# Attention and a softplus layer on one core: q and k transposed by DMA, score halves merged, v in larger packets

## The chip, the cores and the metric

The kernel runs on one core of a Trainium2 chip. The metric is device time in microseconds of one execution; the profile shows one such execution with its engines: TensorE (PE, with PEld for its weight loads), VectorE (DVE), ScalarE (ACT), GpSimd (POOL) and SyncE (SP, which here only issues DMAs).

## The reference

Attention over 768 tokens for 4 batches and 8 heads of 64, where a token sees the first 8 tokens of its batch and the 96 tokens up to itself, with a bias that falls with distance; then a layer 512 to 2048, softplus, and a layer back to 512. Inputs and output are float32.

```python
scores = q @ k.T / sqrt(64)                    # per batch and head
rel = pos[:, None] - pos[None, :]
is_global, is_local = pos[None, :] < 8, (rel >= 0) & (rel < 96)
dist = where(is_global & ~is_local, 96, abs(rel))
scores = where(is_global | is_local, scores - slopes[head] * dist, -1e9)
x = softmax(scores) @ v                        # heads side by side: 3072 x 512
out = softplus(x @ w_in) @ w_out               # 512 -> 2048 -> 512
```

## The kernel before, in words

**Tiles.** The 3072 tokens are 24 blocks of 128; a block `n` attends to itself and the block before it (whose first keys are overwritten by the global ones). Two blocks are a window `w` of 256 tokens, 12 in all, three to a batch. A window's q, k and v are loaded as float32 (`q32`, `k32`, `v32`), cast to bfloat16 (`qb`, `kb`, `vb`), and q and k are transposed to `qT`, `kT`. Two tokens that follow each other in memory lie in one partition of q32 and k32 (512-byte packets); v is loaded by four DMAs of 256-byte packets, which put each token into the partition where the value matmul wants it.

**Stages.** For a half block (4 heads): `scores` (8 matmuls of 64 rows into the two banks of `s_ps`, 4 in the first block of a batch), `add_bias` on VectorE into `z`, `expo` on ScalarE into `pb`, `pv` (8 matmuls into `x_ps`), `normalize` on VectorE into `xs`. In the first four blocks the bias is added by matmuls and ScalarE reads the scores directly (`expo_early`). `xs` is transposed into `XT`: on TensorE for blocks 0 to 5 and the last two, by a DMA transpose for the others (L444). A group `g` of 256 tokens then takes 8 stages `mm1` (8 matmuls each, a bank of `h_ps`, then `softplus_exp` and `softplus_ln` on ScalarE into `g`) and 8 stages `mm2` (4 matmuls each into the two banks of `o_ps`, two for each half of the tokens, `ns`), two output copies on VectorE into `osb`, and stores.

**The order.** Nothing is scheduled by hand: a `Planner` in the file gives each stage an engine, a duration, a rank and the stages and buffers that it waits for, runs this as a list of events, and the instructions are written out in that order (`pl.plan`). Each engine, and each DMA queue, then works through its own list in order and waits by semaphores. `base(n)` is the rank of block `n`, in first-layer stages: 4n - 11 or 4n - 13. A load of window `w` from 4 on waits for a stage of group w - 3. `behind=[chain]` keeps loads in one line on SP. Until 24 us of the plan TensorE runs `filler` matmuls where it has nothing else.

**PSUM** has eight banks: 2 `s_ps`, 1 `x_ps`, 1 `tr_ps` for transposes, 2 `h_ps`, 2 `o_ps` (`alt`).

**Start.** q and k of window 0 are loaded in halves; weights are issued by GpSimd (`w_in_slice`, `w_out_slice`), slices 0 and 1 when k of window 1 has landed (`after_k`), slices 2 and 3 when k of window 2 has. SP issues the loads of windows 2 and 3 only when w_in slice 1, or 3, has landed (`after_weights`).

## Time and profile before

| what | value |
|---|---|
| median of 3 runs (lowest to highest) | 241.35 us (241.02 to 241.90) |
| profiled execution: time, span | 241.96 us, 240.2 us |
| granted TensorE clock, mean | 0.993 |
| busy: PE, PEld, DVE, ACT, POOL | 223.2, 158.3, 126.5, 153.3, 35.3 us |
| DMA packets | 67305, of them 35408 under 512 bytes |
| read from HBM, written | 27.26 MB, 6.29 MB |

The span goes from the first instruction to the last; the time of the execution is 1.8 us longer. Matmuls overlap, so the busy time of TensorE is not its time at work: the distance from one stage's start to the next one's is. A row of the chain or the timeline has its start, its length, the engine, the line of the file, what is written from what, and how many instructions were merged in it. A row of groups ends in busy time and mean nanoseconds of one, and the idle time ahead of it with what ended most of it.

### The profile page before, as it was taken

The numbers are of one execution on the slowest core, as the hardware profiler recorded it, in microseconds if no ns is written. First come the engines' busy times: TensorE is split into PE (matmuls) and PEld (weight loads), VectorE is DVE, ScalarE is ACT, GpSimd is POOL, SyncE is SP. The second block draws the span as 40 slices with busy tenths as digits, with TensorE's granted clock in tenths as the row PEclk, the third lists the DMA queues.
The fourth block names the chain that finished last, engine by engine and source line by source line (L and its number), as shares of the span: only waits on it lengthen the run. The fifth ranks groups of instructions, "written<-read, shape, count | busy, mean of one in ns | idle before, by whom it ended". The sixth has DMA issues, their size and how long they took to land.

```text
span 240.2 us, 5361 instructions
## 1 busy us (share of the span) xinstructions
PE 223.2 (93%) x2206; PEld 158.3 (66%) x2240; DVE 126.5 (53%) x260; ACT 153.3 (64%) x208; POOL 35.3 (15%) x62
## 2 busy tenths in 40 slices
PE   6889985998999979999999999999999999899994
PEld 6678664675867657767667667667667677577643
DVE  6275331379669565745665676457638537420030
ACT  4636535793688657766956866766677678568600
POOL 3252034012222021011022021012022000000000
PEclk9999998899999999999999999999999999999999
DMA  6999999999961663474781852763942302003032
GB/s 177 217 155 187 178 233 189 180 246 245 250 140 25 144 166 89 111 203 98 187 195 23 212 140 47 178 154 85 259 94 64 68 4 68 23 0 90 0 87 89
DMA packets 67305, 31.81 MB, mean 132 GB/s; under 512 B 35408, under 2 KB 64336, under 8 KB 67280
## 3 DMA queue, kind: packets, MB, share of 16 engines
q1 hardware_dynamic: 62912, 27.14, 49.2%
q0 software_dynamic: 4224, 4.19, 11.1%
q8 instruction: 17, 0.28, 0.5%
q10 hardware_dynamic: 144, 0.13, 0.2%
q14 instruction: 8, 0.07, 0.1%
HBM read 27.26 MB, written 6.29 MB: 140 GB/s over the span
## 4 chain that ended last, share of the span: by engine, by line
PE 72%; DVE 11%; DMA 7%; SPq 4%; issue 3%; ACT 1%; POOL 1%; DVEq 0%; POOLq 0%
PE h_ps L454 30%; PE o_ps L482 26%; DVE z L380 5%; PE s_ps L362 5%; PE x_ps L406 3%; DMA k_211<-in_k_dram 3%; PE tr_ps L303 3%; PE o_ps L498 3%; DMA v_593<-in_v_dram 2%; SPq L279 2%; DMA q_1345<-in_q_dram 2%; DVE osb L517 2%; PE alt_d L596 1%; SPq L282 1%; DVE qT L312 1%
## 5 line engine op out<-in xcount | busy, mean ns | idle before, releaser
L454 PE MATMUL h_ps<-XT,w_in_bf 128*128 128x256 bf16 x768 | 98.5, 275 | 0.0
L482 PE MATMUL o_ps<-w_out_bf,g 128*128 128x512 bf16 x320 | 84.9, 379 | 2.7 <-issue 0.8
L454 PEld LDWEIGHTS <-w_in_bf 128*128 128x128 bf16 x768 | 73.1, 99 | 20.0 <-issue 0.2
L464 ACT ACTIVATE e<-h_ps 128x512 f32<-128x512 f32 x96 | 56.4, 591 | 39.1 <-PE h_ps L454 38.7
L386 ACT ACTIVATE pb<-z 128x1024 bf16<-128x1024 f32 (+1 forms) x40 | 39.5, 988 | 22.1 <-DVE z L380 12.6
L468 ACT ACTIVATE g<-e 128x1024 bf16<-128x1024 f32 x48 | 50.6, 1055 | 1.3
L482 PEld LDWEIGHTS <-g 128*128 128x128 bf16 x352 | 31.8, 98 | 25.2 <-ACT g L468 0.7
L380 DVE TENSOR_TENSOR z<-s_ps,biasA 128x1024 f32<-128x1024 f32 x34 | 41.5, 1220 | 13.0 <-PE s_ps L362 9.6
L517 DVE COPY osb<-o_ps 128x512 f32<-128x512 f32 x22 | 14.9, 684 | 17.7 <-PE o_ps L482 17.5
L418 DVE TENSOR_TENSOR xs<-x_ps,rcp 128x256 bf16<-128x256 f32 x48 | 20.4, 424 | 1.7
L417 DVE RECIPROCAL rcp<-x_ps 128x4 f32<-128x4 f32 x48 | 8.5, 178 | 23.7 <-PE x_ps L406 20.4
L362 PE MATMUL s_ps<-qT,kT 64*128 64x128 bf16 x336 | 17.7, 221 | 2.0 <-DVE z L380 1.5
L406 PEld LDWEIGHTS <-pb 128*128 128x128 bf16 x320 | 14.4, 97 | 7.1 <-ACT pb L386 1.5
L362 PEld LDWEIGHTS <-kT 64*128 64x128 bf16 x352 | 10.4, 95 | 10.8 <-issue 8.2
L312 DVE COPY qT<-tr_ps 128x1024 bf16<-128x1024 bf16 x11 | 7.6, 691 | 16.6 <-PE tr_ps L303 16.6
L596 PE MATMUL alt_d<-ident 128*128 128x128 bf16 x128 | 11.6, 244 | 2.3 <-POOL ident masks.py:199 2.3
L312 DVE COPY kT<-tr_ps 128x1024 bf16<-128x1024 bf16 x11 | 7.5, 684 | 8.2 <-PE tr_ps L303 8.0
L328 POOL COPY kT<-kT 128x32 bf16<-128x32 bf16 x16 | 3.6, 223 | 52.3 <-PE s_ps L362 48.1
L596 PEld LDWEIGHTS <-ident 128*128 128x128 bf16 x128 | 9.2, 112 | 2.9 <-POOL ident masks.py:199 2.3
L303 PE MATMUL tr_ps<-ident,kb 128*128 128x128 bf16 x88 | 6.7, 219 | 3.7 <-POOL kb L292 2.7
L303 PEld LDWEIGHTS <-kb 128*128 128x128 bf16 x96 | 6.2, 98 | 4.9 <-POOL kb L292 3.0
L392 ACT ACTIVATE pb<-s_ps 128x512 bf16<-128x512 f32 (+1 forms) x12 | 5.7, 525 | 5.7 <-PE s_ps L362 5.7
(111 smaller groups left out, 140.1 us busy)
## 6 DMA issues: line engine op xcount, KB each, us to landing
out_dram<-osb SPq DMA_DIRECT2D x45, 128.0 KB, 2.5
w_in_bf<-in_moe_w_in_dram POOLq DMA_DIRECT2D x4, 512.0 KB, 7.7
w_out_bf<-in_moe_w_out_dram POOLq DMA_DIRECT2D x4, 512.0 KB, 10.0
q_123<-in_q_dram SPq DMA_DIRECT2D x2, 256.0 KB, 3.7
k_125<-in_k_dram SPq DMA_DIRECT2D x2, 256.0 KB, 4.4
v_129<-in_v_dram SPq DMA_DIRECT2D x4, 128.0 KB, 5.5
q_201<-in_q_dram SPq DMA_DIRECT2D x1, 512.0 KB, 6.3
k_211<-in_k_dram SPq DMA_DIRECT2D x1, 512.0 KB, 7.6
```

Of the source, the lines that this page charges most:

```text
L303: nc.tensor.transpose(tr[:, m - lo, r, :], src[:, r, 2 * m : 2 * m + 2, :].rearrange("p a b -> p (a b)"), ident[:],)
L362: nc.tensor.matmul(banks[sub][:, lh // 2 if i == 0 else 2 * (lh // 2) + b, :], qk_of("k", n - b)[rows, m, :], qT[rows, m, :], start=begin, ...
L380: nc.vector.tensor_tensor(z[:], s_ps[:], biasA[:, half, :, :], ALU.add)
L386: nc.scalar.activation(pb[:, 0:nr, :], z[:, 0:nr, :], AF.Exp, scale=1.0 / root_d)
L406: nc.tensor.matmul(xv[:, lh, :], pb[:, 2 * j + b, :], vb_of(n - b)[:, h, :], start=b == 0, stop=b == 1,)
L418: nc.vector.tensor_tensor(xs[:, 4 * half : 4 * half + 4, :], xv[:, :, 0:D], rcp[:][:, :, None].to_broadcast([P, 4, D]), ALU.mult,)
L454: nc.tensor.matmul(hv[:, j, :], w_in_bf[:, m, fb * P : fb * P + P], XT[:, m, W * g : W * g + W], start=(m == 0), stop=(m == NM - 1),)
L464: nc.scalar.activation(e[:, p % 2, :], state["h", g, p][:], AF.Exp)
L468: nc.scalar.activation(gt[:, 4 * c : 4 * c + 4, :].rearrange("p a t -> p (a t)"), state["e", g, c][:].rearrange("p a t -> p (a t)"), AF.Ln ...
L482: nc.tensor.matmul(state["o", g][ns][:], gt[:, fb, ns * P : ns * P + P], w_out_bf[:, fb, :], start=(fb == 0), stop=(fb == NFB - 1),)
L517: copy_on[eng](osb[:], state["o", g][ns][:])
L596: nc.tensor.matmul(alt["d"][:, 0:P], ident[:], ident[:])
```

## The change

It does four things.

1. From window 4 on (`T_DMA`) q and k are transposed by DMA (`transp_dma`), two transposes each per window, from `qb` and `kb` straight into `qT` and `kT`. k is cast by four instructions of 64 partitions that also move each token to its partition (`cast_by_block`); q keeps its two interleaved halves and is read with a step by `q_of`. Windows 0 to 3 are still transposed on TensorE, into the banks H or O.
2. v is loaded like q and k, in one DMA of 512-byte packets, and its four casts move it.
3. PSUM is dealt out anew: `s_ps` is two pairs of banks (S0, S1), `tr_ps` is gone, `o_ps` is one bank. From block 8 on (`MERGED`) both halves of a block's scores are one stage (`scores_both`), each half in a pair of its own. The second layer runs one half of the tokens after the other in the one bank (`mm2_one`); group 0's second layer runs in S1 (`mm2_first`), which therefore holds no scores meanwhile.
4. Ranks and choices of the planner follow: casts of windows 0 to 3 may go to any of three engines, casts of later windows come 4 ranks earlier, loads of a window wait for an earlier stage.

```diff
-    s_ps = ps.tile([P, 8, P], F32, name="s_ps")
+    s_ps = [ps.tile([P, 8, P], F32, name=f"s_ps{i}") for i in range(2)]
     x_ps = ps.tile([P, 512], F32, name="x_ps")
-    tr_ps = ps.tile([P, 1024], BF16, name="tr_ps")
-    alt = {x: bank(f"alt_{x}", f"bank_{x}") for x in "abcd"}
+    h_ps = [ps.tile([P, 512], F32, name=f"h_ps{i}") for i in range(2)]
+    o_ps = ps.tile([P, 512], F32, name="o_ps")
...
     def load(w, what, heads=slice(0, H)):
         b, ww = divmod(w, WPB)
-        dst = raw_of(what[0], w)
-        if what[0] == "v":
...
-            nc.sync.dma_start(dst[64 * r : 64 * r + 64, blk, :, :], vv[r])
...
+        src = {"q": q, "k": k, "v": v}[what][b, heads, W * ww : W * ww + W, :]
+        dst = raw_of(what, w)[:, heads, :]
+        nc.sync.dma_start(dst, src.rearrange("h (p r) d -> p h (r d)", r=2))
...
+    def cast_by_block(eng, w, what, blk, r):
...
+        src = raw_of(what, w)[64 * blk : 64 * blk + 64, :, r * D : r * D + D]
+        copy_on[eng](dst[64 * r : 64 * r + 64, :, :], src)
...
+    def transp_dma(w, what, i):
+        dst = q_tile(w) if what == "q" else k_tile(w)
+        nc.sync.dma_start_transpose(
+            dst[:, i, :, :], state[what + "b", w][:, i, :, :].rearrange("p h d -> p (h d)")
+        )
...
+    def q_of(n, rows, m):
+
+        b = 64 * (n % 2)
+        return state["qT", n // 2][rows, :, m, b : b + 64]
...
+    def scores_both(n):
+        scores(n, 0, s_ps[0], True)
+        scores(n, 1, s_ps[1], True)
...
+    def mm2_one(g, dst, ns, fbs):
+        for fb in fbs:
+            nc.tensor.matmul(
+                dst,
+                state["g", g][:, fb, ns * P : ns * P + P],
+                w_out_bf[:, fb, :],
+                start=(fb == 0),
+                stop=(fb == NFB - 1),
+            )
...
+    def mm2_first(p, s_t):
         for ns in range(2):
...
+            mm2_one(0, o_first(ns, s_t), ns, range(2 * p, 2 * p + 2))
...
-        {"S": 1, "X": 1, "TR": 1, "H": 2, "O": 1, "e": 3, "g": 3, "osb": 3, "z": 3, "pb": 3,
+        {"S0": 1, "S1": 1, "X": 1, "H": 2, "O": 1, "e": 3, "g": 3, "osb": 3, "z": 3, "pb": 3,
...
-    EARLY = 4
+    EARLY, MERGED, T_DMA = 4, 8, 4
...
-                if early:
+                if w < 4:
                     eng = {"pool": 1.05 * f, "act": 0.2 + 0.85 * f, "dve": 0.1 + 0.6 * f}
...
-                    u - 5.0 + 0.1 * (what == "k"),
+                    u - (5.0 if w < T_DMA else 9.0) + 0.1 * (what == "k"),
...
+                if w >= T_DMA:
+                    for i in range(2):
+                        o = pl.add(
+                            f"D{what}{w}", "sp", 1.2,
+                            lambda op, what=what, i=i: transp_dma(w, what, i), u - 19.0,
+                            after=wait, takes=takes if i == 0 else (), dma=(32, 20), slack=1.5,
+                            frees=free_b if i else (),
+                        )
...
+                elif half == 0:
+                    sc = pl.add(
+                        f"scores{n}", "pe", 2 * pe - 0.18, lambda op: scores_both(n), r,
+                        after=after, takes=(("S0",), ("S1",)),
...
             mm2s[g, p] = pl.add(
-                f"mm2_{g}_{p}", "pe", 0.865, lambda op, g=g, p=p: mm2(g, p), r,
...
+                f"mm2_{g}_{p}", "pe", 0.865,
+                lambda op, g=g, ns=ns, c=c: mm2_one(g, o_ps[:], ns, range(4 * c, 4 * c + 4)),
...
-        for what, p in (("q", 1), ("k", 1), ("v", 4)):
+        for what, p in (("q", 0), ("k", 0), ("v", 2)):
```

How the order moves is not in these lines. Three places matter for what follows. In the rows, numbers tell buffers apart; `x2` is two equal instructions in a row.

SP's queue around the loads of window 10, a middle window: first before, q and k, a half's stores, an x transpose, and v.

```order
L282 DMA q32_2382<-in_q_dram 128x8x128
L282 DMA k32_2394<-in_k_dram 128x8x128
L524 DMA out_0_dram<-osb_2370 64x512 x2
L444 DMA_TRANSPOSE XT_103<-xs_2416 128x4x128
L279 DMA v32_2478<-in_v_dram 64x8x64 x4
L444 DMA_TRANSPOSE XT_103<-xs_2518 128x4x128
L524 DMA out_0_dram<-osb_2601 64x512 x2
```

And now:

```order
L278 DMA q32_2249<-in_q_dram 128x8x128
L278 DMA k32_2253<-in_k_dram 128x8x128
L560 DMA out_0_dram<-osb_2237 64x512 x2
L278 DMA v32_2298<-in_v_dram 128x8x128
L333 DMA_TRANSPOSE qT_2312<-qb_2300 128x4x128 x2
L476 DMA_TRANSPOSE XT_102<-xs_2280 128x4x128
L333 DMA_TRANSPOSE kT_2372<-kb_2331 128x4x128 x2
L560 DMA out_0_dram<-osb_2355 64x512 x2
L476 DMA_TRANSPOSE XT_102<-xs_2396 128x4x128
```

Four transposes stand in the queue behind the window's own loads, and those of k behind a transpose of x; v is one DMA in place of four.

VectorE's queue in the same stretch of the kernel, before: `z` is a half's bias add, `osb` an output copy, `vb` the global rows of v.

```order
L417 RECIPROCAL rcp_2320<-x_ps_80 128x4
L418 TENSOR_TENSOR xs_2267<-x_ps_80,rcp_2320 128x256
L380 TENSOR_TENSOR z_2323<-s_ps_79,biasA_108 128x1024
L517 COPY osb_2345<-o_ps_2120 128x512
L334 COPY vb3_89<-vb1_87 4x8x64 x2
L517 COPY osb_2370<-o_ps_2121 128x512
L380 TENSOR_TENSOR z_2384<-s_ps_79,biasA_108 128x1024
L312 COPY kT_2406<-tr_ps_81 128x1024
```

And now:

```order
L449 RECIPROCAL rcp_2218<-x_ps_81 128x4
L450 TENSOR_TENSOR xs_2162<-x_ps_81,rcp_2218 128x256
L416 TENSOR_TENSOR z_2226<-s_ps0_79,biasA_107 128x1024
L553 COPY osb_2237<-o_ps_84 128x512
L363 COPY vb3_88<-vb1_86 4x8x64 x2
L416 TENSOR_TENSOR z_2261<-s_ps1_80,biasA_107 128x1024
```

The PSUM copies of the transposes are gone, one output copy stands in each block instead of two in every second, and the two adds read different banks.

Window 2 at the start. Before, its v and k were both cast by GpSimd, behind the issue of weights:

```order
L529 DMA w_in_bf_101<-in_moe_w_in_dram 128x4x512
L535 DMA w_out_bf_102<-in_moe_w_out_dram 128x4x512
L289 CAST vb2_88<-v32_593 128x16x64
L292 CAST kb_690<-k32_582 128x1024
L328 COPY kT_710<-kT_209 128x8x4
```

Now VectorE casts all three:

```order
L285 CAST qb_640<-q32_595 128x1024
L320 COPY qT_663<-h_ps0_82 128x1024
L285 CAST kb_675<-k32_603 128x1024
L294 CAST vb2_87<-v32_607 64x8x64 x4
L416 TENSOR_TENSOR z_718<-s_ps0_79,biasA_107 128x1024
L416 TENSOR_TENSOR z_735<-s_ps0_79,biasA_107 128x1024
```

k's cast now stands ahead of v's, and both adds of block 4 behind them; both read the first pair of score banks.

On TensorE the matmuls are the same but for 128 transposes that are gone (and 19 more fillers ahead of the first layer). Score stages, counted as runs of score matmuls, are 29 instead of 48.

More of the change, by code (lines that the diff above doesn't have):

```diff
@@ L706, in attention_window @@
                     lambda op, what=what, ms=ms: transp(w, what, tr_bank(op.taken), ms),
-                    r, after=[c, *(done if what == "k" else ())],
-                    takes=(*((("qT",),) if part == 0 and what == "q" else ()),
-                           ("TR", "O") if early else ("TR",)),
+                    r, after=wait, takes=(*takes, TR),
                 )
@@ L851 @@
                         1000.0 + 4 * part + chunk,
-                        after=[lns[g, chunk], before, copies[0] if part == 2 else None],
-                        takes=(("O",),) if part == 0 and chunk == 0 else (),
+                        after=[lns[g, chunk], before],
+                        takes=((LAST[part][2][0],),) if chunk == 0 else (),
                     )
```

302 lines of the change are left out of this document (174 added, 128 removed).

## The prediction

> **What bounds the kernel now.** I read the page first: engine shares, clock, chain.
>
> ```profile
> PE 72%; DVE 11%; DMA 7%; SPq 4%; issue 3%; ACT 1%; POOL 1%; DVEq 0%; POOLq 0%
> PE h_ps L454 30%; PE o_ps L482 26%; DVE z L380 5%; PE s_ps L362 5%; PE x_ps L406 3%; DMA k_211<-in_k_dram 3%; PE tr_ps L303 3%; PE o_ps L498 3%; DMA v_593<-in_v_dram 2%; SPq L279 2%; DMA q_1345<-in_q_dram 2%; DVE osb L517 2%; PE alt_d L596 1%; SPq L282 1%; DVE qT L312 1%
> ```
>
> The chain is TensorE for 72%. Whether it is full everywhere is a matter of stages, so I asked for stretches (columns: length, busy time of PE, PEld, DVE, ACT, POOL with counts, clock, DMA share, GB/s).
>
> ```profile
> 20.00:40.00 20.00, 16.05 (x174) 12.00 (x176) 5.63 (x16) 11.82 (x18) 5.54 (x9) 1.00 1.13 198
> 40.00:60.00 20.00, 19.21 (x188) 12.72 (x188) 13.13 (x24) 12.86 (x17) 2.58 (x4) 0.91 1.13 220
> 120.00:140.00 20.00, 19.64 (x197) 13.79 (x200) 13.11 (x24) 12.66 (x17) 3.53 (x5) 1.00 0.60 147
> ```
>
> There are two regimes. Up to 60 us the DMA engines are full (share over 1) and TensorE has holes: 4 us in 20 to 40. In the third row, from the middle of the kernel, TensorE is busy 19.6 of 20 and DMA 60%. There a microsecond taken off TensorE's queue is a microsecond of time, as long as no other engine fills up. Third, the timeline of TensorE in the full stretch, because busy time overlaps: what a stage costs is the distance from its start to the start of the next.
>
> ```profile
> 102.58 0.41 PE L406 MATMUL x_ps<-vb_86,pb 128*128 128x65 bf16 x8
> ...
> 102.91 0.29 PE L362 MATMUL s_ps<-qT,kT 64*128 64x128 bf16 x4
> ...
> 103.13 1.04 PE L482 MATMUL o_ps<-w_out_bf,g 128*128 128x512 bf16 x4
> ...
> 110.54 0.61 PE L303 MATMUL tr_ps<-ident,qb 128*128 128x128 bf16 x8
> ...
> 110.99 0.29 PE L403 MATMUL x_ps<-vb_87,pb 128*128 128x65 bf16 x4
> ...
> 114.70 0.40 PE L362 MATMUL s_ps<-qT,kT 64*128 64x128 bf16 x8
> ...
> 115.04 1.05 PE L454 MATMUL h_ps<-XT,w_in_bf 128*128 128x256 bf16 x8
> ...
> 115.92 0.41 PE L406 MATMUL x_ps<-vb_87,pb 128*128 128x65 bf16 x8
> ...
> 116.16 1.03 PE L482 MATMUL o_ps<-w_out_bf,g 128*128 128x512 bf16 x3
> ```
>
> A transpose stage of 8 takes 110.99 - 110.54 = 0.45 us. Eight score matmuls take 115.04 - 114.70 = 0.34 us and four take 103.13 - 102.91 = 0.22: 0.03 for each matmul and 0.10 for leaving the stage. Entering costs as well: eight value matmuls followed by scores take 0.33 (102.58 to 102.91), followed by something else 0.24 (115.92 to 116.16). So each score stage carries about 0.10 + 0.09, or 0.2 us, that doesn't depend on how many matmuls it has.
>
> Fourth, the chain in order of time, for the start.
>
> ```profile
> 7.11 7.64 DMA k_211<-in_k_dram
> ...
> 31.63 5.66 DMA v_593<-in_v_dram
> 37.44 1.04 POOL vb_88 L289
> 38.48 0.99 POOL kb L292
> 39.52 0.62 PE tr_ps L303 x8
> 40.14 3.02 PE h_ps L454 x16
> ...
> 43.70 1.94 PE h_ps L454 x16
> ...
> 110.70 0.46 PE tr_ps L303 x8
> ...
> 162.87 0.46 PE tr_ps L303 x8
> ```
>
> GpSimd casts window 2's v before its k, v is the last load to land, and TensorE's next row is the transpose of that k: it waits 2.7 us, although first-layer matmuls of group 1 stand behind it and were ready. Then 16 matmuls take 3.02 us, against 1.94 a little later: the clock was down (0.91 is the mean of 40 to 60). The wait itself, from the list of waits:
>
> ```profile
> PE tr_ps L303 <- POOL kb L292: 2.7, 1, 2.7
> ```
>
> The last two rows of the chain are the same place three windows apart: (162.87 - 110.70)/3 = 17.4 us for a window of 256 tokens.
>
> **The change, part by part.**
>
> *Transposes off TensorE.* Windows 4 to 11 lose their 16 transposes each: 8 x 2 stages x 0.45 = 7.2 us, all behind 60 us. Nothing takes their place on TensorE. The PSUM copies that followed them on VectorE go too, off the path.
>
> *Score halves merged.* Counted in the order, score stages fall from 48 to 29 with the same 352 matmuls: 19 x 0.2 = 3.8 us. The second half no longer waits for the first half's bias add, since each has its own two banks:
>
> ```profile
> PE s_ps L362 <- DVE z L380: 1.5, 2, 1.2
> ```
>
> I take that 1.5 us as gone; the bounds are 0 and 1.5.
>
> *What must keep up.* Per window the new SP queue issues 3 loads, 4 half stores and 6 transposes (2 of x as before, 4 new).
>
> ```profile
> L444 SPq DMA_TRANSPOSE XT<-xs x16: 1205/1216/1489, 65.2 to 190.4; - x16
> DMA to landing us min/median/max: 2.4/2.4/4.1
> 114.18 1.17 SPq L524 DMA_DIRECT2D out_dram<-osb  x2
> 115.40 0.58 SPq L282 DMA_DIRECT2D q_1851<-in_q_dram  x1
> L292 POOL CAST kb<-k_125 128x512 bf16<-128x512 f32 x1 | 0.6, 616 | 0.9 <-DMA k_125<-in_k_dram 0.9
> k_582<-in_k_dram SPq DMA_DIRECT2D x1, 512.0 KB, 5.5
> ```
>
> That is 3 x 0.58 + 2 x 1.17 + 6 x 1.22 = 11.4 us of a window that should shrink to 17.4 - 2 x 0.45 - 2 x 0.2 = 16.1. The q and k transposes have the shape of the x transposes in the trace, so 1.22 to issue and 2.4 to land is a price for the same operation; two in a row are not in the trace, which bounds each between 1.22 and 2.4 us of queue time. I take 1.22, since other DMAs are issued straight behind a transpose. The path of k is then: landing 5.5, four casts of half the partitions at 0.62 each (bounds 0.31, if half the partitions cost half, and 1.2; GpSimd has the room, 3.5 busy of 20 in the third stretch), two issues 2.4, landing 2.4: 12.8 us. The load may start when group w-3 starts, and the scores of window w stand 11 first-layer stages later by the ranks in the code, 22 us at 16.1/8 a stage. So some 9 us are spare, and I cost it at nothing. If that cover went, scores and every row behind them on TensorE would wait.
>
> *One output bank, ns after ns.* Second-layer stages have the same matmuls; between the halves VectorE must copy the bank. VectorE's queue in the part on the change has each output copy behind a block's first add:
>
> ```profile
> L380 DVE TENSOR_TENSOR z<-s_ps,biasA 128x1024 f32<-128x1024 f32 x34 | 41.5, 1220 | 13.0 <-PE s_ps L362 9.6
> L517 DVE COPY osb<-o_ps 128x512 f32<-128x512 f32 x22 | 14.9, 684 | 17.7 <-PE o_ps L482 17.5
> ```
>
> On TensorE the last stage of one half comes behind the scores, then two first-layer stages (16 matmuls, 1.94 by the chain), then the next half. Add and copy, 1.22 + 0.68 = 1.9, have from the scores' end the 1.94 and one second-layer stage for it. I cost it at nothing (0 to 1 us in all). ScalarE has to fit as well:
>
> ```profile
> L464 ACT ACTIVATE e<-h_ps 128x512 f32<-128x512 f32 x96 | 56.4, 591 | 39.1 <-PE h_ps L454 38.7
> L386 ACT ACTIVATE pb<-z 128x1024 bf16<-128x1024 f32 x34 | 35.7, 1051 | 12.7 <-DVE z L380 12.6
> L468 ACT ACTIVATE g<-e 128x1024 bf16<-128x1024 f32 x48 | 50.6, 1055 | 1.3
> ```
>
> 8 x 0.59 + 4 x 1.05 + 4 x 1.06 = 13.2 us a window: under 16.1, so TensorE stays the bound.
>
> A page speaks against this step: the Trainium skill, "VectorE: DVE Perf Modes", section "Rules for kernel authors", says to transpose 128x128 on TensorE where a PSUM destination will do, and its table of three paths gives the DMA crossbar 1309 ns against 390. By that price alone 128 blocks would lose 128 x 0.92 = 118 us (an estimate from that table), by the rows they gain 7.2, since the queue that pays has 5 us a window to spare.
>
> *v in 512-byte packets.* Of the chain before 62 us, where DMA is full, this is what moves.
>
> ```profile
> 28.04 0.51 SPq L282 DMA_DIRECT2D k_582<-in_k_dram  x1
> L529 POOL DMA_DIRECT2D w_in_bf<-in_moe_w_in_dram x4: 747/762/888, 14.9 to 35.2; - x4
> DMA to landing us min/median/max: 5.6/7.7/10.1
> ```
>
> k of window 2 landed at 28.04 + 5.5 = 33.5, and v at 31.63 + 5.66 = 37.3: 3.7 us for as many bytes as k, weights beside it. An even share for k would be nearer 2, so v costs up to 1.7 us too much; I take half, 0.8, for each v ahead. The first-layer matmuls wait for the first weight slice (14.9 + 5.6 = 20.5), and that was issued when k_211 had landed (7.11 + 7.64 = 14.75). One v is ahead of k_211, another beside the weights: the start moves 1.0 us earlier (0 to 2.5).
>
> *Window 2's casts.* k is now cast on VectorE, ahead of v, so the 2.7 us wait and the slow 1.1 us (3.02 - 1.94) go. Two things come: block 4's two halves both go through the first pair of score banks, because the second pair holds group 0's output, so the second half waits for the first's add (1.22 plus about 0.4 to be seen); and that add stands on VectorE behind v's four casts, which wait for v's landing. I put the new wait at 2.0 us: net -1.8. Bounds: -3.8 when the wait hides, +0.5 when it lasts 3.2 and slows the clock again.
>
> The Trainium skill, "TensorE: Matmul & The Clock Gate", section "Why this matters for your kernels", asks for no idle gap over about 3 us; the trace has the slower clock behind one of 2.7. By either, a wait of 2.0 costs only itself.
>
> **Sum.** 7.2 + 3.8 + 1.5 + 1.0 + 1.8 = 15.3 us. The profiled execution took 241.96, 0.6 above the median of the runs, 241.35. So 226.7 against the one and 226.0 against the other, which is the time that I predict. All good ends: 7.2 + 3.8 + 1.5 + 2.5 + 3.8 = 18.8, or 222.5 against the median. All bad ends: 7.2 + 3.8 - 0.5 - 1.0 = 9.5, or 231.9.
>
> **Rivals.** *Late inputs.* SP is one queue in order, and a transpose of x waits there for its block to be normalised while the k transposes and the next loads stand behind it. Between 55 and 75 us, where two windows' transposes are issued for the first time, q, k and v of window 5 stand in one line with them. For it: even now loads come late at times.
>
> ```profile
> DVE qb L292 <- DMA q_1345<-in_q_dram: 4.0, 1, 4.0
> ```
>
> Against it: 9 us spare. If half of the spare time is lost and 1 us of waiting is left in each of eight windows, 234. Chance 0.16.
>
> *Transposes follow one another only when landed.* Then each takes 2.4 of SP: 6 x 2.4 + 1.7 + 2.3 = 18.4 us a window. SP becomes the bound of eight windows: 226.0 + 8 x (18.4 - 16.1) = 244, slower than before. It decides from the place where a transpose costs 2.3 us of queue (window 18.0, 226.0 + 8 x 1.9 = 241.2). Against it: other DMAs follow a transpose after 1.2. Chance 0.05. The Trainium skill's table of transpose paths ("VectorE: DVE Perf Modes", "The three transpose paths"), paid in queue time, would end on this side too.
>
> *Something else holds the window at 17.4*, and the time only loses the start, 238 to 241: ScalarE at 13.2 and SP at 11.4 leave no room for it. Chance 0.03.
>
> **How the numbers follow.** The forecast (222 to 231) has 0.76. Its bounds, a microsecond wider below for other loads that now come late, make the range, 221.5 to 232; with the near part of the first rival (a waiting of 0.7 us a window still ends at 232) it holds 0.8. Half a per cent, 1.2 us, is about what a measurement can tell here. Faster: 0.76 + 0.16 + half of the last rival = 0.93; within it 0.02; slower 0.05.
>
> **What would show it.** Right: in the middle of the kernel the distance of one window's first scores to the next's is 16.1 us; no transposes on TensorE behind 60 us; score stages of 16 that take 0.6; SP queue rows of transposes 1.2 apart; first-layer matmuls start before 20.2. Wrong: TensorE idle ahead of scores with a DMA of qT or kT as releaser; SP rows of transposes 2.4 apart; waits of TensorE on the output copy; a clock below 1 behind 45 us.

## The result and the profile after

| | before | after |
|---|---|---|
| median of 4 runs (lowest to highest) | 241.62 us (241.02 to 242.32) | 234.11 us (233.01 to 235.50) |
| ratio to before, 95% interval | | 0.969 (0.963 to 0.976) |
| profiled execution: time, span | 241.96, 240.2 us | 234.69, 232.9 us |
| granted TensorE clock, mean | 0.993 | 0.976 |

The change takes off 7.5 us. The prediction said 15.3 and 226.0, range 221.5 to 232: the time is 2.1 us above the range. Two of the four runs had a mean clock of 0.976 (234.69 and 235.50 us), the other two 0.993 (233.01 and 233.53); the profile is of the first. Chips differ by half a per cent in the runs below, so kernels are compared by their ratio to before on the same chip; the medians there are of all four runs, while the ratios leave out two executions in a slower state, 563.79 us of gpsimd_stores_earlier_loads and 235.78 us of order_alone, whose only profile is therefore not used.

The page of after, clock and DMA share in 40 slices of 5.8 us:

```profile
PEclk9999999999999799976999999999999999999999
DMA  6979899999955896695497595895995112101112
```

Slices 14 (75.7 to 81.5 us), 18 and 19 (99 to 110.6) ran at a lower clock; before had one, the 8th (42.0 to 48.0). Three stretches of after, with the columns of the prediction's first stretches:

```profile
60.00:80.00 20.00, 17.33 (x165) 11.77 (x163) 11.89 (x23) 13.34 (x19) 6.56 (x13) 0.91 0.77 159
100.00:120.00 20.00, 16.67 (x136) 10.31 (x135) 9.21 (x19) 11.16 (x16) 5.10 (x9) 0.83 0.79 192
120.00:140.00 20.00, 20.00 (x194) 14.04 (x193) 13.99 (x26) 16.05 (x21) 9.21 (x18) 1.00 0.91 175
```

From 120 to 140 us TensorE is busy 20.0 of 20 (19.6 before). The first two stretches have holes of 2.7 and 3.3 us, where before was busy 19.4 and 19.7, while the DMA engines are at 77 to 79%, not full. Where the two kernels stand against each other shows in the timeline of TensorE, first matmuls of group 5 and of group 10; before:

```profile
112.42 1.04 PE L454 MATMUL h_ps<-XT,w_in_bf 128*128 128x256 bf16 x8
...
199.16 1.04 PE L454 MATMUL h_ps<-XT,w_in_bf 128*128 128x256 bf16 x8
```

and after:

```profile
112.37 1.04 PE L486 MATMUL h_ps_82<-XT,w_in_bf 128*128 128x256 bf16 x8
...
192.85 1.04 PE L486 MATMUL h_ps_82<-XT,w_in_bf 128*128 128x256 bf16 x8
```

At 112 us nothing is won. The gain comes behind it: five windows in 80.5 us in place of 86.7 (6.3 of the 7.3 us between the profiled executions; the last 1.0 lies behind group 10's first matmul), so a window takes 16.10 in place of 17.35. That is the prediction's 16.1. What was to be won by 112 us is lost in two places, which the list of TensorE's waits names (total, times, longest):

```profile
PE o_ps L509 <- DVE osb L553: 4.1, 2, 3.3
PE h_ps_82 L486 <- DMA XT<-xs: 2.7, 1, 2.7
...
PE s_ps_79 L385 <- DVE z L416: 1.3, 1, 1.3
```

*The first place.* TensorE's timeline, with the wait in brackets:

```profile
70.72 0.39 PE L385 MATMUL s_ps_80<-qT,kT 64*128 64x128 bf16 x8
73.77 1.05 PE L486 MATMUL h_ps_82<-XT,w_in_bf 128*128 128x256 bf16 x8 [2.67 <-DMA XT<-xs]
...
74.90 1.78 PE L486 MATMUL h_ps_83<-XT,w_in_bf 128*128 128x256 bf16 x8
76.48 1.91 PE L486 MATMUL h_ps_82<-XT,w_in_bf 128*128 128x256 bf16 x8
78.18 0.53 PE L438 MATMUL x_ps<-vb_89,pb 128*128 128x65 bf16 x8
```

Group 3's first stage waits 2.8 us for the DMA transpose of block 7's x. (The text counts a wait from start to start, less the usual step; brackets and lists count from the modelled end of the matmul ahead and are 0.1 to 0.2 shorter.) Behind the wait two stages take 1.58 and 1.70 (start to start) where such a stage takes 0.87: another 1.5 us at half clock. Why the transpose was late, the timeline of SyncE's queue tells:

```profile
47.38 1.53 SPq L278 DMA_DIRECT2D q_865<-in_q_dram  x1
...
54.36 1.68 SPq L278 DMA_DIRECT2D k_984<-in_k_dram  x1
56.09 3.52 SPq L560 DMA_DIRECT2D out_dram<-osb  x2
59.72 2.62 SPq L333 DMA_TRANSPOSE qT<-qb  x2
62.44 2.53 SPq L333 DMA_TRANSPOSE kT<-kb  x2
65.06 1.22 SPq L476 DMA_TRANSPOSE XT<-xs  x1
66.45 3.44 SPq L333 DMA_TRANSPOSE qT<-qb  x2
69.98 1.21 SPq L333 DMA_TRANSPOSE kT<-kb  x1
71.30 1.21 SPq L476 DMA_TRANSPOSE XT<-xs  x1
...
95.61 1.56 SPq L278 DMA_DIRECT2D q_1545<-in_q_dram  x1
```

Every row begins where the one ahead ends, or at most 0.5 us later. The issues between 47.3 and 97.2 add up to 47.1 us of the 49.9; in before they add up to 31.8. From 47 to 56 us issuing a load takes 1.5 to 1.7 us, not the 0.58 of the prediction. Two shorter stretches, with the same columns:

```profile
47.00:58.00 11.00, 11.00 (x117) 8.16 (x117) 8.23 (x16) 8.60 (x14) 2.83 (x5) 1.00 1.21 298
66.00:74.00 8.00, 5.33 (x63) 3.27 (x62) 5.27 (x9) 3.75 (x4) 0.42 (x2) 1.00 0.58 89
```

In the first the DMA engines are full, and loads are issued at the pace of their bytes: five of 512 KB from 47.38 to 56.09 are 301 GB/s. In the second the engines stand at 58%, and SyncE is issuing nearly all the time: what is late there is late by the queue. Block 7's x was written at 66.0 and its transpose issued at 71.30, behind three of window 5's.

*The second place.* TensorE, and then VectorE, whose bracket names the load that it stands for:

```profile
99.14 1.04 PE L486 MATMUL h_ps_83<-XT,w_in_bf 128*128 128x256 bf16 x8
103.51 1.86 PE L509 MATMUL o_ps<-w_out_bf,g 128*128 128x512 bf16 x4 [3.33 <-DVE osb L553]
105.41 1.90 PE L486 MATMUL h_ps_82<-XT,w_in_bf 128*128 128x256 bf16 x8
107.10 1.91 PE L509 MATMUL o_ps<-w_out_bf,g 128*128 128x512 bf16 x4
108.80 1.21 PE L486 MATMUL h_ps_83<-XT,w_in_bf 128*128 128x256 bf16 x8
```

```profile
94.53 0.42 DVE L450 TENSOR_TENSOR xs<-x_ps,rcp 128x256 bf16<-128x256 f32 x1
101.02 0.69 DVE L285 CAST qb<-q_1545 128x1024 bf16<-128x1024 f32 x1 [6.06 <-DMA q_1545<-in_q_dram]
...
102.18 0.68 DVE L416 TENSOR_TENSOR z<-s_ps_79,bias_106 128x512 f32<-128x512 f32 x1
102.78 0.68 DVE L553 COPY osb<-o_ps 128x512 f32<-128x512 f32 x1
```

The load of window 7's q was issued at 95.61 (the last row of SyncE above) and landed at 101.0. VectorE stood 6.1 us in order at its cast; the copy that frees the one output bank is four rows further on. TensorE waited 3.5 us and then ran about 5 us slowly, some 2.7 us lost. Together: 2.8 + 1.5 + 3.5 + 2.7 = 10.5 us.

### The profile page after: what moved, and what is told of

The parts are those of the page before. It is cut to its first block, busy times and chain, and to the rows that moved or that the text cites. A ratio compares the mean times of both kernels' runs of the same rounds, so it can differ in the third digit from the quotient of the medians.

```text
span 232.9 us, 5214 instructions
## 1 busy us (share of the span) xinstructions
PE 218.2 (94%) x2131; PEld 153.9 (66%) x2131; DVE 120.2 (52%) x251; ACT 156.7 (67%) x209; POOL 56.5 (24%) x111
## 4 chain that ended last, share of the span: by engine, by line
PE 90%; DVE 4%; DMA 3%; issue 1%; POOL 1%; SPq 0%; POOLq 0%; DVEq 0%
PE o_ps L509 30%; PE h_ps_83 L486 19%; PE h_ps_82 L486 17%; PE x_ps L438 4%; PE o_ps L632 4%; PE s_ps_79 L385 3%; PE s_ps_80 L509 3%; DMA q_1545<-in_q_dram 2%; PE s_ps_80 L385 2%; PE o_ps L534 2%; DMA XT<-xs 1%; PE h_ps_82 L311 1%; DVE z L416 1%; DVE osb L553 1%; PE s_ps_80 L534 1%; PE s_ps_79 L534 1%
## 5 line engine op out<-in xcount | busy, mean ns | idle before, releaser
L486 PEld LDWEIGHTS <-w_in_bf 128*128 128x128 bf16 x768 | 74.9, 99 | 25.1 <-DMA XT<-xs 2.8
L509 PE MATMUL o_ps<-w_out_bf,g 128*128 128x512 bf16 x320 | 83.3, 386 | 4.1 <-DVE osb L553 4.1
L486 PE MATMUL h_ps_83<-XT,w_in_bf 128*128 128x256 bf16 x400 | 52.9, 276 | 0.0
L486 PE MATMUL h_ps_82<-XT,w_in_bf 128*128 128x256 bf16 x368 | 49.5, 279 | 2.7 <-DMA XT<-xs 2.7
L496 ACT ACTIVATE e<-h_ps_83 128x512 f32<-128x512 f32 x50 | 29.8, 595 | 28.7 <-PE h_ps_83 L486 28.7
L496 ACT ACTIVATE e<-h_ps_82 128x512 f32<-128x512 f32 x46 | 27.2, 591 | 11.3 <-PE h_ps_82 L486 11.1
L416 DVE TENSOR_TENSOR z<-s_ps_79,biasA 128x1024 f32<-128x1024 f32 x19 | 23.1, 1218 | 3.2 <-PE s_ps_79 L385 3.2
L553 DVE COPY osb<-o_ps 128x512 f32<-128x512 f32 x20 | 13.7, 685 | 18.5 <-PE o_ps L509 18.3
L416 DVE TENSOR_TENSOR z<-s_ps_80,biasA 128x1024 f32<-128x1024 f32 x15 | 18.3, 1222 | 0.3
L632 PE MATMUL o_ps<-ident 128*128 128x128 bf16 x147 | 13.6, 244 | 2.3 <-POOL ident masks.py:199 2.3
L632 PEld LDWEIGHTS <-ident 128*128 128x128 bf16 x147 | 10.9, 111 | 3.5 <-POOL ident masks.py:199 2.3
L385 PE MATMUL s_ps_79<-qT,kT 64*128 64x128 bf16 x196 | 10.2, 219 | 1.3 <-DVE z L416 1.3
L509 PE MATMUL s_ps_80<-w_out_bf,g 128*128 128x512 bf16 x32 | 8.2, 379 | 0.0
L385 PE MATMUL s_ps_80<-qT,kT 64*128 64x128 bf16 x156 | 7.9, 216 | 0.0
```

Source lines behind the costliest of these rows:

```text
L385: nc.tensor.matmul(s_t[:, 4 * sub + (lh // 2 if i == 0 else 2 * (lh // 2) + b), :], k_of(n - b, rows, m), q_of(n, rows, m), start=begin, s ...
L416: nc.vector.tensor_tensor(packed(n, z), rows_of(n, s_t), bias, ALU.add)
L486: nc.tensor.matmul(hv[:, j, :], w_in_bf[:, m, fb * P : fb * P + P], XT[:, m, W * g : W * g + W], start=(m == 0), stop=(m == NM - 1),)
L496: nc.scalar.activation(e[:, p % 2, :], state["h", g, p][:], AF.Exp)
L509: nc.tensor.matmul(dst, state["g", g][:, fb, ns * P : ns * P + P], w_out_bf[:, fb, :], start=(fb == 0), stop=(fb == NFB - 1),)
L553: copy_on[eng](osb[:], src)
```

## The experiments

The theories: **A**, SyncE's one queue is late from 47 to 97 us, and rows in order behind it, on SyncE and on VectorE, turn that into waits of TensorE, each followed by a slow clock. **B**, the transposes or the bytes are late in themselves, in any order. **C**, the parts of the change bring less than thought. **D**, the clock falls for reasons of its own. **E**, one output bank is too little.

| kernel | median, before on the same chip | ratio (95%) |
|---|---|---|
| the change | 234.11, 241.62 | 0.969 (0.963 to 0.976) |
| x7_ahead | 232.58, 240.83 | 0.964 (0.960 to 0.969) |
| kept_busy | 233.88, 240.83 | 0.970 (0.965 to 0.975) |
| two_windows_on_tensor | 229.43, 240.83 | 0.952 (0.946 to 0.958) |
| sp_prices | 231.04, 240.83 | 0.959 (0.954 to 0.964) |
| x7_and_q7 | 230.84, 242.34 | 0.957 (0.947 to 0.967) |
| all_on_tensor | 235.78, 242.34 | 0.974 (0.967 to 0.981) |
| halves_apart | 236.02, 242.34 | 0.976 (0.967 to 0.984) |
| earlier_loads | 227.85, 242.34 | 0.940 (0.934 to 0.947) |
| stores_on_gpsimd | 224.97, 242.38 | 0.931 (0.924 to 0.937) |
| earlier_loads_4 | 236.00, 242.38 | 0.975 (0.969 to 0.981) |
| gpsimd_stores_earlier_loads | 229.96, 242.38 | 0.947 (0.940 to 0.953) |
| v_as_before | 234.17, 242.38 | 0.966 (0.961 to 0.971) |
| stores_moved_alone | 231.50, 241.47 | 0.956 (0.950 to 0.963) |
| order_alone | 231.83, 241.47 | 0.957 (0.950 to 0.964) |
| gpsimd_stores_tail | 223.30, 241.47 | 0.925 (0.922 to 0.929) |

### One row moved on SyncE

`behind` puts steps of the plan, named with their place among steps of the same name, directly behind another:

```diff
     plan = pl.plan({"pe": 2.4, "dve": 4.5, "act": 2.1, "pool": 3.2, "sp": 0.7, "none": 0.0})
+    behind([("Dq5", 0), ("Dq5", 0), ("Dk5", 0)], "DX7")
```

> SyncE's order alone is changed: the transpose of block 7's x is issued ahead of both q transposes and the first k transpose of window 5; nothing else moves. Theory A (order on SyncE's one queue, and a half clock behind each long wait of TensorE): the wait of 2.9 us at 70.9 goes and with it the slow stretch behind it (8 matmuls in 1.7 us in place of 0.87, twice), so TensorE is 4.6 us ahead at 80 us. What is left at the end depends on SyncE: if it has slack behind 74 us, 229.5; if its queue is the bound up to 98 us, the load of window 7's q stays where it is, the wait at 99.9 (3.5 us) grows by what was won, and the time is 232 to 234. Theory B (the transposes by DMA, or the bytes, are late in themselves, whatever their order): the wait comes back at block 10's scores, 234.

The wait at 70.9 is gone with its slow stretch. The time moves by half a per cent, and the intervals overlap: the load of window 7's q still leaves at 95.98, and TensorE, which now comes earlier, waits in other places. Behind 24 us its list of waits in x7_ahead is headed by:

```profile
PE o_ps L509 <- DVE osb L553: 3.6, 3, 1.7
```

That is A's second case in its time: up to 96 us the queue is the bound, and a wait that is taken away comes back. It is not in the form that I expected: the wait at 99.9 didn't grow, it became 1.9 us at 102.4, and others came. In this execution 2.1 us were also lost by 56 us, ahead of the rows that moved (group 2's first matmul at 55.87, in the change at 53.76): block 4's second half waited 2.1 us with half clock behind it, where the change waited 1.5 without. The other three runs had a clock of 0.993 for 0.984 and took 232.15 to 232.67, so the time doesn't hang on this.

### The clock behind a wait

```diff
     def mm1(g, p, turn):
         state["h", g, p] = h_ps[turn]
+        if (g, p) == (3, 0):
+            for _ in range(48):
+                nc.tensor.matmul(h_ps[turn][:, 0:P], ident[:], ident[:])
```

> 48 matmuls of ident by ident (128x128) are put in TensorE's queue ahead of group 3's first first-layer stage, in the bank that this stage fills next, so they run inside the wait of 2.9 us at 70.9; their result is thrown away. Theory A says that the slow stretch behind the wait is the price of the idle time, about 1.7 us of its own: the wait stays as long, the stages behind it take 0.87 and TensorE is 1.7 us ahead at 80 us (232.4 at the end, or 234 if the second wait takes it back). Theory D (the clock falls for another reason, load or time): the stages behind the wait still take 1.6 to 1.7 and the time is 234 to 236.

TensorE's timeline of kept_busy:

```profile
71.58 2.85 PE L484 MATMUL h_ps<-ident 128*128 128x128 bf16 x48
74.52 1.05 PE L489 MATMUL h_ps<-XT,w_in_bf 128*128 128x256 bf16 x8
75.41 0.41 PE L438 MATMUL x_ps<-vb,pb 128*128 128x65 bf16 x8
75.65 1.91 PE L489 MATMUL h_ps<-XT,w_in_bf 128*128 128x256 bf16 x16
77.39 0.41 PE L438 MATMUL x_ps<-vb,pb 128*128 128x65 bf16 x8
```

The two stages that took 3.3 us take 1.74 (75.65 to 77.39). The slow stretch is the price of standing idle; D falls. The time stays (0.970): window 7's q was issued at 96.5, and its wait, 2.9 us, took the gain back.

### Less in the queue where it is full

```diff
-    EARLY, MERGED, T_DMA = 4, 8, 4
+    EARLY, MERGED, T_DMA = 4, 8, 6
```

> q and k of windows 4 and 5 are transposed on TensorE as before the change; windows 6 to 11 stay with the DMA. Theory A: eight transposes of 1.3 us leave SyncE's queue just where it is behind, between 59 and 74 us; TensorE takes 4 stages of 0.45 = 1.8 us more, and both long waits with their slow stretches (2.9 + 1.7 + 3.5 + 1.7 = 9.8) go or shrink to a third: 226 to 229. Theory C (the waits come from the merged score stages or from the DMA's bytes, not from the queue): nothing but the cost, 236.

0.952: some 4 us faster than the change (229.4 us, just above A's range), though TensorE does four transpose stages more. One long wait is left, of 2.4 us at 81.7, again VectorE at the cast of a q. C's 236 falls. Its order is the planner's for this kernel, and this holds for the next one too.

```diff
+    FULL = [(3, "v"), *((w, x) for w in (4, 5) for x in "qkv")]
...
         dur, dma = 0.55 * f + 0.05, (64 * f, 28)
+        if (w, what) in FULL:
+            dur = 1.7
```

> The planner that sets the order is told what the trace shows of SyncE: 1.7 us for each load of v of window 3 and of windows 4 and 5 (0.6 before), 1.3 for a transpose (1.2 before). It then puts window 5's k and v loads behind window 4's q transposes, and block 7's x ahead of all of window 5's transposes. Same work on every engine. Theory A: transposes of window 4 are issued 3 us earlier, the first wait goes, the second shrinks: 226 to 230. Theory B: 233 to 235.

0.959, or 231.4 at the 241.35 us from which the forecast was made, a little above A's range. Two waits of 2.4 us are left, each with 1.4 us of slow clock behind it. Telling the planner the true price of an issue brings about a third of what was lost; window 7's q was still issued only at 92.3.

### The cast on VectorE, and the single bank

On top of x7_ahead:

```diff
     behind([("Dq5", 0), ("Dq5", 0), ("Dk5", 0)], "DX7")
+    behind([("castq7", 0), ("Dq7", 0)], "oc3_0")
```

> On top of block 7's x ahead of window 5's transposes, the cast of window 7's q (and its first transpose) stands on VectorE behind the first add of block 12 and the output copy, no longer ahead of them. Theory A says that TensorE's wait for the output copy at 102.4 (1.9 us there, 3.5 in the changed kernel, half clock behind it) is nothing but this cast standing in order for a load that lands at 101: it goes, and 232.6 becomes 229 to 230, unless the transposes of window 7, which are late by the same load, then hold block 14's scores. Rival E (the single output bank is too little in itself): the wait for the copy stays, 232 to 233.

The wait at 102 is gone, though TensorE gets there earlier (at 101.8, in x7_ahead at 102.5), so it was the cast, and not the bank, that made it. In halves_apart, below, the same cast holds up a bias add in this way, for 3.3 us by the list, and not the output copy. In the profiled execution another wait grew in place of this one, to 3.9 us at 78.4: VectorE's output copy waits for a buffer, because the half stores that free it stand in SyncE's queue until 75.40. The list of VectorE's waits:

```profile
DVE osb L553 <- DMA out_dram<-osb: 5.5, 1, 5.5
```

The time, 0.957 with a wide interval, can't tell 229 from 232. E holds for the short waits, 0.8 us by the list at 89 us and at the end of the change, and not for the long one.

### What the parts are worth

```diff
-    EARLY, MERGED, T_DMA = 4, 8, 4
+    EARLY, MERGED, T_DMA = 4, 8, 99       # all_on_tensor
+    EARLY, MERGED, T_DMA = 4, 24, 4       # halves_apart
```

> No q or k is transposed by the DMA; score stages merged, v in 512-byte packets and moved by the casts as in the change. By the prediction's own terms the change without the transposes takes off 3.8 + 1.5 + 1.0 + 1.8 = 8.1 us: 233 against 241. Theory A (the DMA transposes are worth their 7.2 in the steady part and lose 9.8 between 70 and 110 us): 231 to 234, no wait of over 1 us between 60 and 120 us, a window of about 17.1. Theory C (the merged halves bring little): 237 or more.

> The two score halves of blocks 8 to 23 are two stages again, as before the change; DMA transposes and v's loads stay. 16 stages come back at 0.2 us each: +3.2, up to +4.7 if the wait of the second half for the first's add comes back too. By the prediction's terms the window becomes 16.1 + 0.4 = 16.5 to 16.6. With the two long waits as they are, 237 to 239; if part of it falls into the waits, 235.

First-layer matmuls of groups 5 and 10, all_on_tensor:

```profile
108.65 1.04 PE L486 MATMUL h_ps<-XT,w_in_bf 128*128 128x256 bf16 x8
...
195.14 1.04 PE L486 MATMUL h_ps<-XT,w_in_bf 128*128 128x256 bf16 x8
```

and halves_apart:

```profile
112.31 1.04 PE L486 MATMUL h_ps<-XT,w_in_bf 128*128 128x256 bf16 x8
...
194.95 1.04 PE L486 MATMUL h_ps<-XT,w_in_bf 128*128 128x256 bf16 x8
```

A window takes 86.5/5 = 17.30 without the DMA transposes and 82.6/5 = 16.53 with the halves apart, against 16.10 for the whole change and 17.35 before. What each part is worth depends on the other: the transposes bring 0.82 a window with the halves apart and 1.20 with them merged (0.9 predicted), merging brings 0.05 with the transposes on TensorE and 0.43 with them on the DMA (0.4 predicted). Together they bring 1.25 (1.3 predicted), so in the steady part nothing is missing, and C falls there. That merging alone hardly moves the window fits a wait in all_on_tensor: its transposes borrow banks of the first layer, and six times TensorE waits up to 0.4 us behind them for a bank. By its ratio all_on_tensor takes 235.1 of 241.35 us, 1 us more than I expected at most.

It also has a wait that I had excluded (none over 1 us between 60 and 120). TensorE, then VectorE in all_on_tensor:

```profile
83.16 1.02 PE L509 MATMUL o_ps<-w_out_bf,g 128*128 128x512 bf16 x3 [2.02 <-DVE osb L553]
80.13 0.69 DVE L285 CAST qb<-q 128x1024 bf16<-128x1024 f32 x1 [4.44 <-DMA q<-in_q_dram]
```

Half clock follows it. VectorE stands at the cast of window 6's q. The load of that q was issued at 74.12, behind two half stores and a transpose of x, although SyncE had issued nothing for 6.6 of the 7.8 us from 63.79 to 71.61. So a cast that stands too early in VectorE's order costs TensorE a wait without a full queue too; in the change it stood longer (6.1 us for 4.4). A is right about the order, and the full queue is not the only reason for a late load.

```diff
+        if what == "v" and w < 3:      # four DMAs of 256-byte packets, one whole cast
+            for blk in range(2):
+                ...
+                for r in range(2):
+                    nc.sync.dma_start(dst[64 * r : 64 * r + 64, blk, :, :], vv[r])
```

> v of windows 0, 1 and 2 is loaded in four DMAs of 256-byte packets and cast whole, as before the change; the rest is the changed kernel. The prediction gave v's packets 1.0 us of the start (0 to 2.5) and a part of window 2's 1.8. First-layer matmuls start at 21 in place of 20, k of window 1 and the first slice of weights land 1 to 2 us later; the time is 234 to 236. If the start was worth nothing, or all of it is lost again in the queue behind, 233 to 234.

The ratio is that of the change within its interval. k of window 1 lands at 14.2 (13.0 in the change, 14.7 before) and the first weights at 19.95 (18.9, 20.6), yet the first-layer matmuls start at 20.12, against 20.09 in the change (20.62 before): in the change it is the rows ahead of them on TensorE that are in the way. Something is lost behind the start all the same: group 2's first matmul comes at 57.83 (53.76 in the change), group 5's only 0.7 late. That fits the other half of the expectation, a loss that the late queue hides, but doesn't show it, for the planner's order differs too.

### Earlier loads

```diff
-                o.wait_for(mm1s[w - 3, p])
+                o.wait_for(mm1s[w - 3, p] if w < 6 else mm1s[w - 4, p + 4])
     # and LAST: part 0 in S0, part 1 in S1, part 2 in O
```

> On top of windows 4 and 5 transposed on TensorE: the loads of windows 6 to 11 may start half a group (8 us) earlier, and the last group's first output goes through a score bank, so that the output bank need not be free for it. Theory A: the one long wait that is left in that kernel, 2.4 us at 81.7 behind the cast of a q that lands late, goes, and 0.9 at the end: 229.4 - 2.4 - 0.9 = 226.1, range 225 to 227.5. If the earlier loads collide with others in the DMA, 228 to 230.

> The changed kernel with all its DMA transposes, the loads of windows 6 to 11 allowed half a group earlier, and the last output through a score bank. Theory A: SyncE's queue is as full as before up to 90 us, so the loads come earlier only by pushing transposes and stores back; the wait at 99.9 for the cast of q goes, the one at 70.9 stays (2.9 + 1.6): 234 - 3.5 - 2.7 - 0.9 = 227 at best, 231 if the queue takes it back in another place. I expect 230, above the 227 to 228 of the kernel with windows 4 and 5 on TensorE.

Both kernels also put the last group's first output through a score bank (the edit shown at gpsimd_stores_tail), and earlier_loads has windows 4 and 5 on TensorE. That one reaches 0.940, with no wait over 1.9 us behind 24 us and no slow clock. With all transposes on the DMA the same edit is no gain over the change (0.975 for 0.969, intervals overlapping), and I had expected 230. Its loads leave earlier and fill the DMA engines again (a share of 1.06 from 77 to 85 us), and a group of four half stores behind them takes 5.7 us to issue; SyncE in earlier_loads_4:

```profile
77.60 1.79 SPq L278 DMA_DIRECT2D v<-in_v_dram  x1
79.44 5.69 SPq L560 DMA_DIRECT2D out_dram<-osb  x4
```

### Room on the queue, or the order in it

```diff
-            nc.sync.dma_start(dst[r], osb[64 * r : 64 * r + 64, :])
+            nc.gpsimd.dma_start(dst[r], osb[64 * r : 64 * r + 64, :])
...
-                f"store{g}_{ns}", "sp", 1.15, ...
+                f"store{g}_{ns}", "pool", 1.2, ...
```

> Against the changed kernel, the half stores of the output are issued from GpSimd's queue and no longer from SyncE's: the same bytes, 14 fewer issues of about 0.6 (one pair took 3.5) between 56 and 97 us on SyncE, some 10 us. All transposes of q and k stay with the DMA. In five kernels so far the load of window 7's q was issued at 95.6 to 96.5, wherever TensorE stood. Theory A (SyncE's queue is the bound from 47 to 96 us): that load is now issued at 85 to 88, the waits of 2.9 and 3.5 go or shrink to half, 227 to 230. Theory B (bytes of the DMA are the bound): the load stays at 93 or later and the time at 232 to 235. A cost of its own: GpSimd waits for the output copies ahead of its casts of k and v, up to 1 us a window where that shows.

0.931, better than expected. Two stretches, and the longest wait of TensorE behind 24 us:

```profile
60.00:80.00 20.00, 19.73 (x184) 12.81 (x181) 13.76 (x26) 13.81 (x19) 11.83 (x22) 1.00 1.15 224
80.00:100.00 20.00, 19.94 (x213) 14.49 (x212) 12.98 (x26) 17.61 (x25) 9.00 (x17) 1.00 0.98 187
```

```profile
PE s_ps L385 <- DVE z L416: 1.7, 1, 1.7
```

The DMA engines moved 224 GB/s in the stretch where they moved 159 in the change: the bytes were not the bound there, the queue that asks for them was. From 56 us on B falls. Ahead of that, from 47 to 56 us, the loads are issued at the same 1.5 to 1.7 us as in the change, and there the bytes do set the pace. Window 7's q leaves at 90.03, 5.6 us earlier, though not at the 85 to 88 expected. The Trainium skill, "DMA: Bandwidth & Descriptors", section "Issuing engines are not separate DMA queues", says that issuing from a second engine saves only the issuing engine's time, usually small beside the transfer. The runs agree that this is what is saved; here it was on the path, and with the new order 3.8% of the time hung on it. The planner also wrote a new order for this kernel, so two more runs part the two: the first edit alone with the change's own order, and the second alone with the stores left on SyncE.

> The changed kernel with its own order on every engine, word for word, but for the half stores of the output, which are issued by GpSimd at the same places of the program. If room on SyncE's queue is what was short (theory A): the queue is 4 us ahead at 60 us and 10 us ahead at 96, window 7's q is loaded at 86 to 89, the wait at 99.9 goes, that at 70.9 shrinks from 2.9 to below 1 although block 7's x still stands behind window 5's transposes: 225 to 228. If the order is what helped, the time stays at 232 to 235.

> The order that the planner wrote for the kernel with the stores on GpSimd, but with the stores issued by SyncE at the places where that order has them. Theory A: the queue is as full as in the changed kernel, 232 to 236, window 7's q loaded at 95 or later, waits of 2 us and more between 60 and 110. If the order is what helped: 225 to 228.

| | the change's order | the new order |
|---|---|---|
| stores from SyncE | 0.969 | 0.957 |
| stores from GpSimd | 0.956 | 0.931 |

Neither is the cause alone, and both expectations missed: each gives about 3 us, and the two together 9. The 3 of the stores is probably too little: in the profiled execution of stores_moved_alone 2.5 us are lost by 56 us, ahead of the first store (group 2's first matmul at 56.28, in the change at 53.76), again behind a longer wait of block 4 with half clock; three runs have this clock (0.985) and 231.5 us, the fourth 0.991 and 229.52. With room but the old order, the wait for block 7's x is as long as in the change. The one pair of stores ahead of it had taken 3.5 us because the DMA was full; without it the next pair of transposes takes 4.5. Window 7's q is loaded at 94.6 all the same, for SyncE now waits from 82.9 to 85.4 for the cast of window 6's q. The wait at 99.9 is gone. The longest that is left in stores_moved_alone:

```profile
PE h_ps L486 <- DMA XT<-xs: 2.8, 1, 2.8
```

Which rows of the new order do their part once there is room I have not taken apart; it has block 7's x ahead of window 5's k, like x7_ahead.

> Both of the others together: stores from GpSimd's queue and earlier loads, all transposes of q and k by the DMA. If SyncE's queue was the only thing in the way, this is the change as it was predicted: no wait of TensorE over 2 us, no half clock behind 45 us, 225 to 227 (the prediction's 226.0). If GpSimd, now waiting for output copies, is late with k's or v's casts, 228 to 231.

0.947, not the 225 to 227 us expected: the earlier loads cost here too, and waits for the output copy are back (3.1 us in three). They helped only where the transposes of windows 4 and 5 are out of the way, and about 1 us of that step (0.952 to 0.940) can be the last output's.

```diff
-        (0, slice(0, DM), ("O", 0)),
-        (1, slice(0, DM // 2), ("S0", 0)),
-        (1, slice(DM // 2, DM), ("S1", 0)),
+        (0, slice(0, DM), ("S0", 0)),
+        (1, slice(0, DM // 2), ("S1", 0)),
+        (1, slice(DM // 2, DM), ("O", 0)),
```

> The kernel with the stores on GpSimd's queue, and the last group's first output through a score bank, so that TensorE need not wait for the output bank's last copy. In that kernel the wait is 0.95 us at 211.4 with nothing behind it but the tail: 225.0 becomes 224.0, ratio to before 0.926 to 0.927. If the tail is bound by the copies and stores behind it, no change.

0.925, 223.3 us, the fastest kernel of this study: 18 us under before. The wait at the end is gone from the trace; the step from 0.931 is of the size expected, but the two intervals overlap.

## Why the prediction was wrong

*The step that failed* is "What must keep up", where queue and cover were "costed at nothing". The sum 11.4 of 16.1 us is right for a window of the steady part. For the stretch from 47 to 97 us its prices are too low: the 39 issues there come to 33.5 of 49.9 us by them (10 loads at 0.58, 12 half stores at 0.585, 17 transposes at 1.22) and took 47.1. The loads took 6.5 us more, six of the ten 1.5 to 1.7 each, the stores 3.7 more and the transposes 3.4. With that the queue had no room left, and what stood late in its order stayed late. The profile of before held the row that speaks against 0.58, a load issued while the DMA is full, and I took the price from a row where it isn't:

```profile
50.85 2.12 SPq L282 DMA_DIRECT2D q_881<-in_q_dram  x1
```

*The cover* was worked out for the path of k alone. There it held: k of window 7 was issued at 97.22, its last transpose landed at 109.47 (12.3 us, predicted 12.8), and block 14's scores started at 110.94, so 1.5 of the 9 us were left. What broke were its neighbours in the same queues, block 7's x on SyncE and the output copy on VectorE, which have no such cover.

*One output bank*, also at nothing (0 to 1): 4.1 us of waits for the copy by TensorE's list, all but 0.8 of it through the cast of q, and another 0.8 at the end.

*The clock.* A wait was priced at its own length. The waits of 2.8 and 3.5 us cost 1.5 and 2.7 more. The 10.5 us of both places are more than the 8.0 that the profiled executions fall short (15.3 - 7.3). Of the other 2.5, 1.0 was won behind group 10's first matmul (from there to the end of the span 41.0 us before, 40.0 after); the rest I have not settled.

*Transposes off TensorE*, *merged halves*: right together, 1.25 us a window for 1.3. The runs that take them apart show that they are not simply added: by whether the other part is there, the transposes bring 0.82 or 1.20 (0.9 forecast) and merging 0.05 or 0.43 (0.4). The 1.5 us of waits for the first half's add are gone from the list, but for block 4's.

*The start* by v's packets, 1.0: k and the first weights land 1.8 and 1.7 us earlier than before, but the first-layer matmuls no earlier than with v loaded as before (20.09 and 20.12). In the profiles of the other kernels with this start they begin between 18.9 and 20.8, so one execution doesn't settle the term; v_as_before shows no time lost without it at the end, though 4.1 us at group 2.

*Window 2's casts*: the new wait of block 4's second half was 1.5 us (2.0 forecast), without slow clock behind it, and the old 2.7 is gone. Right here; in other kernels with the same casts that wait was 1.5 to 2.4 us, in two of them (x7_ahead, stores_moved_alone) with half clock behind it.

*The rivals.* Late inputs had the place, window 5 and the stretch from 55 to 75 us, and the mechanism, one queue in order; its price, 1 us in each of eight windows, was spread wrongly, though its 234 is what was measured. That the two agree is chance. Its 0.16 was too small for a queue that I had summed only at its steady prices. Transposes one after another only when landed: refuted, two are issued in 2.5 to 2.6 us where the DMA is not full. The window held at 17.4: refuted.

Of the signs named, the right ones showed (a window of 16.1; transposes 1.3 apart; first-layer matmuls at 20.09), and so did two of the wrong ones: waits on the output copy, and a clock below 1 behind 45 us.

That the sum as a whole was sound once the queue is put right, stores_on_gpsimd bears out: 0.931 of 241.35 is 224.6, inside the range and 1.4 under the forecast. It bears out the total, not each term; the start's 1.0 us in particular stays open.

## What to carry to other kernels

A queue that is busy 70% of a steady period can be the bound for 50 us at the start of it: sum its issues between two fixed times of the trace, at the price that an issue has in that stretch, before costing more work on it at nothing. For each instruction that may come late, go through everything behind it in order on its queue and its engine, not only its own consumer. Removing a wait on an engine that runs ahead of a late queue only moves the wait: first give the queue room, then the order that uses it.

## What the runs showed that I had not expected

Issuing a 512 KB load from SyncE took 0.57 to 0.59 us at best (at 73.9, 78.3, 83.0 and 97.2 us of the change) and 1.5 to 1.7 with several loads outstanding, and the queue stood still meanwhile. The same half stores took 1.04 us a pair from GpSimd's queue and 1.17 from SyncE's; in stores_on_gpsimd:

```profile
60.86 1.04 POOL L560 DMA_DIRECT2D out_dram<-osb  x2 [0.29 <-DVE xs L450]
```

The clock: waits of TensorE of 2.2 to 3.9 us were followed by half clock, with one exception (2.4 us in two_windows_on_tensor; the profile of order_alone has one more, of 2.3). The granted clock stood at half for 3.4 us, in three cases for 6.8 (75.0 to 78.4 and 102.3 to 109.2 us in the change), beginning at most 1.4 us after the wait's end, and cost some 1.2 to 2.9 us. Of four waits of 2.0 to 2.1 us one was (x7_ahead, at 36). Shorter ones were not, but for 1.7 and 0.4 us close together at 84 in x7_ahead. The prediction knew only one such case, of 2.7. The Trainium skill, "TensorE: Matmul & The Clock Gate", section "Why this matters for your kernels", asks for no gap above about 3 us; in this kernel gaps from 2.2 us were enough.
